# Fused attention and MLP on one Trainium2 core: turning the row sums with one or two DMAs, zeros through TensorE at the start, and a re-searched instruction order

## The chip, the core and the metric

The kernel runs on one core of a Trainium2 chip. The core has a matrix engine (TensorE, PE in the profile), a vector engine (VectorE, DVE), a scalar engine (ScalarE, ACT), GpSimd (POOL) and SyncE (SP). SyncE computes nothing here: it issues nearly all DMAs, one after the other, and SPq in the profile is its queue of issues. The metric is device time in microseconds (us) of one execution; lower is better.

## The reference, cut to what matters

Attention over 4 batches of 8 heads, 768 positions, 64 numbers per head, and then an MLP on its output. Three heads ("retrieval") see all earlier positions, the five others ("streaming") see a window of 64 and the first 4 positions ("sinks").

```python
scores = scale * np.matmul(q, k.transpose(0, 1, 3, 2))        # (4, 8, 768, 768)
mask = np.where(retrieval_head, causal, causal & (is_sink | in_window))
a = np.exp(np.where(mask, scores, -1e9) - max)
a = a / (np.sum(a, axis=-1, keepdims=True) + 1e-09)           # the row sums
x = np.matmul(a, v)  ->  (3072, 512)
h = x @ w_in                                                  # (3072, 2048)
g = h * (1.0 / (1.0 + np.exp(-beta * h)))
out = g @ w_out                                               # (3072, 512)
```

## The kernel before

**Units.** The work is cut into 8 units of 384 query rows: unit n is half u = n % 2 of batch b = n // 2. For each unit:

- q and k are loaded, cast to bf16 and turned so that the head's 64 numbers lie along the partitions. Units 0 to 2 turn them on TensorE (`transposes`); units 3 to 7 load whole blocks of 128 rows (`load_block`, tile `wf`), cast them on GpSimd (`cast_block`, tile `c`) and turn them by DMA (`turn_block`, the rows `DMA_TRANSPOSE QK<-c`, three per unit).
- `scores`: TensorE multiplies K by Q into PSUM (`sp`), `exps` (ScalarE) writes the exponentials `es`, `masks` (VectorE) zeroes what is masked.
- The row sums: matmuls of `es` with a 0/1 matrix that puts the sum of head h into one row of a PSUM bank. The bank has four groups of 32 rows (`QUARTERS` says which heads go into which group).
- From unit 2 on the sums take this way: `sums_d` (TensorE), `sums_copy` (PSUM to `sc`, mostly ScalarE), `sums_turn` (SyncE, DMAs `rec<-sc` that turn one row of 384 sums into 12 partitions of 32), `recips_d` (VectorE, RECIPROCAL `rec<-rec` of 96x32), `spread_w` (DMA `rd<-rec` to DRAM), `spread_r` (DMAs `R<-rd`, which spread each head's row over 64 partitions).
- `pv`: TensorE multiplies the exponentials by V; `norm` (VectorE) multiplies by `R` and writes `xT`.
- The MLP: `mm1` is 16 steps of 4 matmuls (`b<-xT,w_in`) for the first product, each followed by `swish_a` (ScalarE, tanh, tile `t`) and `swish_b` (VectorE, tile `gT`); `mm2` is 48 matmuls (`b<-w_out,gT`), in pieces of mostly 3, for the second. `out_copy` and `out_store` bring the result out (`osb`).

PSUM has a ring of four banks (`b`) and a ring of two double banks (`sp`). A bank of `mm1` is free again when its `swish_b` is done.

**Order.** No engine reorders anything: every engine runs its instructions in the order in which the program lists them. That order comes from a planner inside the kernel (`_Plan`), which is run once while the program is built. Each piece of work has an engine (or a choice of two), a cost in us, what it needs and gives, the buffers it takes and drops, and a number that ranks it (table `KEYS` per unit, `WEIGHTS` for constants and weights). The planner keeps a clock for each engine and one for the DMA bus, and lets the piece go next that can start first, the rank deciding between equals. For a DMA it says when the data has landed:

```python
            if dma:
                bus = max(bus, t + 0.5) + dma
                end = bus + 1.9
```

`GATES` holds back the loads of units 4 to 7 until a step of `mm1` of an earlier unit. `fill` puts matmuls that nothing reads into the gaps that the planner foresees on TensorE in unit 0; before, they multiply `ident`, which GpSimd and VectorE make first.

`sums_turn` finds runs of neighbouring rows within each group of 32 and issues one DMA for each run: 4 DMAs for an even unit, 6 for an odd one. The planner counts the two cases as 1.2 and 2.1 us of SyncE, and the landing does not hang on that cost.

All instructions are issued through one wrapper, so that the profile gives line 97 for nearly all of them; the tiles tell them apart.

Of the kernel before, what the change touches and what calls it, by code (L numbers as in the profile page):

```python
# [20 lines left out]
NQ = 384  # L21
# [4 lines left out]
RD = 2  # L26

QUARTERS = [[[1, 0], [2, 3], [4, 5], [6, 7]], [[0], [2], [6], [1, 3, 4, 5, 7]]]
# [3 lines left out]
    0: dict(lq=[-165.82, -155.72, -191.56, -178.1], lv=-145.25, C=[-65.39, -131.87, -41.89, -86.23],  # L32
            T=[-109.96, -88.07, -75.65, -67.05], Q=[-124.12, -146.02, -158.63, -111.34],
            cv=[-109.51, -97.53, -83.51], vs=-53.78, vk=-41.5,
            B=[-171.91, -59.89, -207.95, -67.25, -159.55, -110.28],
            E=[-142.81, -104.85, -52.78, -71.02, -207.86, -95.09],
            M=[-53.11, -45.88, -146.62, -152.03, -119.89, -106.16], S=-59.43, PV=[-123, -87.28], X=-92.41,
            F=[-125.92, -113.74, -33.78, -38.27], G=[11.96, 26.88, -25.34, -2.08], H=-153.06, sb=-40.97,
            K=[-58.1, -167.89, -89.9]),
    1: dict(lq=[-152.51, -123.51, -105.94, -134.66], lv=-99.01, C=[-154.83, -128.04, -9.58, -43.56],  # L40
            T=[-55.41, -182.82, -90.82, -169.77], Q=[-57.13, -132.73, -146.37, -81.96],
            cv=[-116.44, -38.55, -150.04], vs=-86.92, vk=-176.99,
            B=[-111, -108.66, -43.08, -108.9, -127.65, -131.33, -50.32, -14.84, -72.5, -21.72, -31.87],
            E=[-129.13, -134.44, -75.3, -47.48, -146.38, -120.46, -64.22, -105.37, -86.8, -132.54, -52.04],
            M=[-145.43, -115.22, -24.07, -114.07, -90.59, -74.79, -21.74, -185.38, -44.07, -45.06, -103.18],
            S=-126.37, PV=[-94.57, -58.91], X=-46.47, F=[-65.81, 2.22, 13.77, -8.12], G=[22.7, 27.98, 33.64, 49.4],
            H=-97.43, sb=-115.4),
    2: dict(lq=[-32.34, 36.54, -11.23, -37.8], lv=21.15, C=[21.76, 11.26, -63.87, 8.43],
            T=[-8.17, -63.33, -9.18, -36.89], Q=[-77.34, -70.04, -74.1, -11.35], cv=[-3.16, 145.7, 184.27], vs=-0.61,
            vk=19.6, B=[-74.54, -33.32, 1.69], E=[-49.81, -78.93, -15.93], M=[-72.26, 2.59, 8.17], S=-31.69,  # L50
            PV=[-16.56, -12.55], X=-38.15, F=[35.42, 13.85, -71.4, 21.4], G=[29.86, 37.66, 64.38, 29.32], R=-84.72,
            K=[-23.72, -47.63, 38.74]),
    3: dict(lq=[23.68], lv=34.32, C=[77.98, -33.67, 15.45], T=[-84.21, -89.69, 27.29], Q=[-43.91, -30.77, 1.18],
            cv=[104.3, 50.32, 139.71], vs=42.23, vk=26.7, B=[-53.03, 29.98, -28.16, -37.77, 10.22, 4.83],
            E=[-14.1, -109.92, 21.88, -3.59, -53.97, -8.41], M=[20.61, 15.21, -101.39, -28.76, 42.21, -8.5],
            S=-25.99, PV=[-52.29, 15.39], X=1.64, F=[-11.21, -21.04, 59.39, 24.49], G=[50.31, 79.24, 78.85, 95.19],
            R=-55.88),
    4: dict(lq=[0.64], lv=72.19, C=[-185.84, 18.49, -88.24], T=[51.44, -0.36, -78.85], Q=[30.04, -109.4, 26.76],
            cv=[9.73, -29.73, 29.61], vs=-1.89, vk=-78.57, B=[3.16, -9.02, -8.62], E=[-83.78, 54.42, 25.91],
            M=[37.95, 3.78, 19.61], S=47.2, PV=[68.33, 74.41], X=95.05, F=[79.33, 77.62, 52.17, 81.21],  # L60
            G=[100.92, 90.46, 90.81, 122.12], R=59.63, K=[-79.06, 20.85, -57.69]),
    5: dict(lq=[-54.23], lv=41.02, C=[-30.79, -100.17, 18.04], T=[-83.52, -0.48, -92.08], Q=[-76.69, -62.07, 36.64],
            cv=[-4.25, 32.39, 34.09], vs=72.24, vk=22.86, B=[27.07, 60.21, 46.43, -4.09, 55.17, -17],
            E=[50.88, -80.34, -97.23, -10.62, -15.3, 15.32], M=[83.6, -25.66, 72.38, 57.39, 68.27, -18.07], S=-7.32,
            PV=[88.41, 70.24], X=25.45, F=[93.13, -7.52, 67.58, 105.49], G=[112.06, 162.66, 102.69, 165.88],
            R=-23.19),
    6: dict(lq=[71.77], lv=-38.06, C=[-52.91, -57.88, 33.52], T=[56.65, -66.66, 25.11], Q=[-0.48, 30.2, -72.44],
            cv=[114.59, 24.4, 118.72], vs=61.5, vk=-61.89, B=[30.8, 69.89, 63.92], E=[45, -9.65, 73.65],
            M=[25.73, 56.3, 69.63], S=22.31, PV=[51.83, 110.46], X=52.04, F=[89.21, 129.45, 134.18, 72.91],
            G=[221.97, 189.97, 171.77, 186.22], R=134.28, K=[-4.2, 53.02, 30.27]),  # L70
    7: dict(lq=[77.55], lv=33.7, C=[-63.72, 57.49, 135.17], T=[-74.45, -13.02, -50.08], Q=[-15.93, -1.82, 53.36],
            cv=[38.13, 102.79, -30.27], vs=170.92, vk=47.74, B=[64.28, -10.97, 44.28, -0.69, 65.07, 43.28],
            E=[-97.6, 7.48, -19.53, 39.61, -51.31, -12.41], M=[161.75, 134.38, -44.81, 3.6, 63.97, 41.6], S=86.05,
            PV=[123.5, 45.3], X=51.72, F=[115.9, 95.83, 106.35, 147.7], G=[152.64, 132.66, 103.11, 188.88], R=-29.36),
}
WEIGHTS = dict(li=[-109.35, -92.93, -97.63, -84.5], lo=[-60.41, -56.12, -88.76, -77.95],
               ci=[-66.33, -100.62, -61.95, -70.77], co=[-53.12, -5.13, -24.02, -40.24], mask=[-76.97, -136.12],
               esel=-109.74, sel=-114.05, sink=-109.74, table=-90.21, masks=-135.98, beta=-73.84)
GATES = [32, 46, 56, 66]
# [23 lines left out]
class _Plan:  # L103
# [16 lines left out]
    def run(self):  # L120
# [11 lines left out]
        while any(left.values()):  # L132
# [62 lines left out]
def kernel(  # L195
# [69 lines left out]
    low = consts.tile([128, 1], F32, name="low")  # L265
    warm = consts.tile([128, 1], F32, name="warm")
# [24 lines left out]
    def const_masks():  # L291
        pool.memset(mask_c, 1.0)
        aff(mask_c, -1, 1, 0, 128)
        pool.memset(odd, 1.0)
        aff(odd, -1, 1, W, W)
        aff(odd, 1, -1, -1, W)
        pool.memset(even, 1.0)
        aff(even[0:W], -1, 1, 0, W)
        aff(even[W:2 * W], 1, -1, -1, W)

# [155 lines left out]
    def load_beta():  # L456
        held["beta"] = rp.tile([FO, 128], F32, name="beta", bufs=1)
        act.dma_start(out=held["beta"], in_=moe_beta.rearrange("(fo fi) -> fo fi", fi=128))
# [149 lines left out]
    BURST_COST = [[0.33, 0.36, 0.75], [0.33, 0.33, 0.4, 0.5, 0.65, 0.18]]  # L608
# [39 lines left out]
    def sums_d(x):  # L648
# [4 lines left out]
        for heads in QUARTERS[x.u]:  # L653
            ops = []
            for h in heads:
                e8 = esel[:, XH.index(h), :, :].rearrange("p a b -> p (a b)")
                if RETR[h]:
                    ops += [(e8, q0, n, e) for (kb, q0, n, e) in x.work[h]]
                else:
                    ops.append((e8, 0, NQ, x.work[h]))  # L660
            if not all(RETR[h] for h in heads):
                ops.append((esel_k.rearrange("p a b -> p (a b)"), q1, NQ - q1, x.esk[0:96, q1:NQ]))
            assert ops[0][1:3] == (0, NQ)
            todo.append(ops)
# [35 lines left out]
    def spread_r(x):  # L700
        x.R = rp.tile([128, NP, NQ], F32, name="R", bufs=RINGS["R"])
        src = x.rd[:]
        for i in range(2):
            sp.dma_start(
                out=x.R[i * D:(i + 1) * D],
                in_=bass.AP(src.tensor, src.offset + i * NQ, [[0, D], [2 * NQ, NP], [1, NQ]]))
# [114 lines left out]
    def attention(n, key, early):  # L821
# [15 lines left out]
        if n >= TD:  # L837
            for i in range(2):
                add(key["lq"][0] + 0.1 * i, "sp", 3.0, lambda i=i: load_block(x, i), dma=3.9, needs=gate,
# [5 lines left out]
            for j in range(TU):  # L845
                add(key["T"][j], "sp", 1.25, lambda j=j: turn_block(x, j), dma=0.7,
# [4 lines left out]
        for j in range(TU):  # L851
# [3 lines left out]
            elif j == 0:  # L855
                add(key["lv"], "sp", 3.0, lambda: [load_v(x, j, sp) for j in range(TU)], dma=3.9, needs=gate,
# [199 lines left out]
```

## Time and profile before

| what | us |
|---|---|
| runs: median of 3 (lowest, highest) | 256.96 (255.67, 258.22) |
| the profiled execution | 256.75 |
| its span, first to last instruction | 255.0 |
| TensorE busy | 230.1 (90%) |
| ScalarE busy | 143.9 (56%) |
| VectorE busy | 139.3 (55%) |
| GpSimd busy | 74.8 (29%) |
| packets of SyncE's hardware queue, share of 16 engines' span | 72.3% |

The span leaves 1.7 us of the execution's time outside. In the rows of a timeline stand the start, the length of the stretch that was merged into the row, the engine, the tiles (out<-in) with their shape, the count, and in brackets how long the engine stood idle before it and who released it. In a table of windows each engine has its busy time and its count of instructions, and PEclk is the share of full clock that TensorE was granted.

### The profile page before, as it was taken

Reading aid. Unit: us, or ns where it says so; the run is one execution under the profiler, and the core shown is the slowest. Engines: PE = TensorE matmul, PEld = TensorE weight load, DVE = VectorE, ACT = ScalarE, POOL = GpSimd, SP = SyncE. Lnnn points to the kernel's source line nnn. Section 1 sums busy time; section 2 is a strip of 40 time slices with the busy share of each in tenths; the row PEclk is TensorE's granted clock in tenths of the full one; section 3 lists DMA queues with packets and bytes.
Section 4 is the critical chain, followed back from the end, with each engine's and each line's share of the span. In section 5 each row is a group of like instructions: output and inputs, shape, how many; then the busy total and the mean of one; then the engine's idle time right before and its main releaser. Section 6 shows DMA issues by size and latency. Waiting matters only on the chain.

```text
span 255.0 us, 5440 instructions
## 1 busy us (share of the span) xinstructions
PE 230.1 (90%) x2103; PEld 125.5 (49%) x2103; DVE 139.3 (55%) x308; ACT 143.9 (56%) x239; POOL 74.8 (29%) x166
## 2 busy tenths in 40 slices
PE   3887999899989999699779959999999899999994
PEld 3645575555435454355334535555544446555441
DVE  4799798787005648236455726637753356566000
ACT  2698957794046974436467326518895254666110
POOL 6245857795800351124124300256000000000000
PEclk9999999999999999999999997999999999999999
DMA  7999999999776985999989929997216033101122
GB/s 204 265 319 316 205 337 332 362 216 195 134 171 197 229 167 121 193 181 238 183 172 211 197 40 155 220 223 194 47 17 154 31 99 85 41 0 43 41 82 82
DMA packets 91119, 42.72 MB, mean 167 GB/s; under 512 B 74693, under 2 KB 83925, under 8 KB 91093
## 3 DMA queue, kind: packets, MB, share of 16 engines
q1 hardware_dynamic: 89973, 41.58, 72.3%
q10 hardware_dynamic: 1120, 0.79, 1.0%
q8 instruction: 16, 0.26, 0.4%
q14 instruction: 10, 0.08, 0.1%
HBM read 31.99 MB, written 6.37 MB: 150 GB/s over the span
## 4 chain that ended last, share of the span: by engine, by line
PE 50%; DMA 21%; SPq 14%; POOL 6%; DVE 4%; issue 2%; ACT 2%; DVEq 0%; POOLq 0%; ACTq 0%
PE b L97 44%; SPq L97 14%; PE sp L97 6%; DMA wf<-in_moe_w_in_dram 6%; DMA wf<-in_v_dram 4%; DMA q2f<-in_q_dram 4%; DMA rec<-sc 3%; DMA wf<-in_moe_w_out_dram 3%; POOL w_out L97 2%; POOL vb L97 1%; DMA QK<-c 1%; DVE gT L97 1%; POOL w_in L97 1%; POOL vs L97 1%; ACT t L97 1%
## 5 line engine op out<-in xcount | busy, mean ns | idle before, releaser
L97 PE MATMUL b<-xT,w_in 128*128 128x384 bf16 x512 | 92.3, 330 | 5.0 <-DVE gT L97 4.4
L97 ACT ACTIVATE t<-b,beta_h 128x384 f32<-128x384 f32 x128 | 73.3, 582 | 37.1 <-PE b L97 23.6
L97 PE MATMUL b<-w_out,gT 128*128 128x512 bf16 x384 | 91.5, 380 | 1.6 <-DVE gT L97 1.6
L97 DVE SCALAR_TENSOR_TENSOR gT<-t,b 128x384 bf16<-128x384 f32 x128 | 69.0, 550 | 27.7 <-ACT t L97 22.2
L97 PEld LDWEIGHTS <-w_in 128*128 128x128 bf16 x512 | 49.3, 99 | 43.1 <-issue 10.0
L97 ACT ACTIVATE es<-sp 128x768 bf16<-128x768 f32 (+1 forms) x68 | 50.6, 793 | 18.1 <-PE sp L97 17.8
L97 PEld LDWEIGHTS <-gT 128*128 128x128 bf16 x384 | 35.7, 98 | 42.7 <-issue 2.5
L97 POOL CAST c<-wf 128x256 bf16<-128x256 f32 x60 | 23.0, 426 | 48.2 <-DMA wf<-in_q_dram 31.4
L97 ACT ACTIVATE osb<-b 128x512 f32<-128x512 f32 x18 | 10.6, 596 | 37.2 <-PE b L97 35.6
L97 PE MATMUL sp<-QK 64*64 64x128 bf16 (+6 forms) x420 | 19.8, 245 | 8.3 <-DMA QK<-c 5.5
L97 PEld LDWEIGHTS <-QK 64*64 64x64 bf16 (+1 forms) x420 | 10.6, 104 | 20.4 <-issue 14.4
L97 DVE TENSOR_TENSOR es<-es,mask_s 128x768 bf16<-128x768 bf16 (+1 forms) x24 | 13.3, 566 | 12.8 <-ACT es L97 12.4
L97 POOL CAST vb<-wf 128x512 bf16<-128x512 f32 x18 | 10.7, 616 | 27.1 <-DMA wf<-in_v_dram 27.1
L97 DVE TENSOR_TENSOR xT<-sp,R 128x768 bf16<-128x768 f32 x12 | 11.1, 954 | 12.5 <-PE sp L97 9.5
L97 PE MATMUL sp<-es,vb 128*64 128x64 bf16 (+3 forms) x228 | 15.6, 241 | 0.0
L97 DVE TENSOR_TENSOR es<-es,mask_c 128x256 bf16<-128x256 bf16 (+2 forms) x32 | 11.9, 389 | 5.7 <-ACT es L97 5.2
L97 DVE RECIPROCAL rec<-rec 96x32 f32<-96x32 f32 x6 | 2.1, 349 | 20.3 <-DMA rec<-sc 20.3
L97 POOL CAST w_in<-wf 128x512 bf16<-128x512 f32 x16 | 10.0, 666 | 8.6 <-DMA wf<-in_moe_w_in_dram 8.6
L97 PEld LDWEIGHTS <-vb 128*64 128x64 bf16 x228 | 11.8, 111 | 1.2
L97 PE MATMUL sp<-es,vs 128*64 128x64 bf16 x120 | 11.0, 196 | 0.0
L97 POOL CAST w_out<-wf 128x512 bf16<-128x512 f32 x16 | 10.0, 676 | 2.7 <-DMA wf<-in_moe_w_out_dram 2.6
L97 PEld LDWEIGHTS <-vs 128*64 128x64 bf16 x120 | 9.2, 111 | 1.6 <-issue 1.4
(74 smaller groups left out, 136.1 us busy)
## 6 DMA issues: line engine op xcount, KB each, us to landing
out_dram<-osb SPq DMA_DIRECT2D x24, 256.0 KB
wf<-in_v_dram SPq DMA_DIRECT2D x18, 256.0 KB
R<-rd SPq DMA_DIRECT2D x12, 384.0 KB
wf<-in_moe_w_out_dram SPq DMA_DIRECT2D x4, 1024.0 KB
wf<-in_q_dram SPq DMA_DIRECT2D x15, 256.0 KB
wf<-in_k_dram SPq DMA_DIRECT2D x15, 256.0 KB
wf<-in_moe_w_in_dram SPq DMA_DIRECT2D x4, 768.0 KB
q2f<-in_q_dram SPq DMA_DIRECT2D x12, 192.0 KB
```

The costliest lines, as they stand in the source:

```text
L97: ins = f(*a, **k)
```

## The change

**The sums' rows at constant steps.** `QUARTERS` and the new `ROWS` place head i of a group at row 16*i (even units) or row i (odd units) of its group of 32; the sums of an even unit then lie at rows 0, 16, 32, ... 112, one constant step, and those of an odd unit at 0, 32, 64 and 96 to 100. One DMA turns the first, two the second. The heads' order in `rec` and `rd` becomes `ORDER`; for odd units `spread_r` then needs three DMAs where two did. In the 0/1 matrix `one` (a window of which puts a sum into any row) and `own_k` (the sinks' part) take the place of `esel` and `esel_k` from unit 2 on; the first two units keep the old ones, and `own_k` is made on VectorE by three memsets and ten small casts.

```diff
-QUARTERS = [[[1, 0], [2, 3], [4, 5], [6, 7]], [[0], [2], [6], [1, 3, 4, 5, 7]]]
+QUARTERS = [[[1, 0], [2, 3], [4, 5], [6, 7]], [[2], [6], [0], [3, 5, 7, 1, 4]]]
+ROWS = [16, 1]
+ORDER = [[1, 0, 2, 3, 4, 5, 6, 7], [2, 6, 0, 3, 5, 7, 1, 4]]
...
         x.rec = rp.tile([8 * CR, 32], F32, name="rec")
-        for g, heads in enumerate(QUARTERS[x.u]):
-            at = sorted(XH.index(h) for h in heads)
-            while at:
-                n = 1
-                while n < len(at) and at[n] == at[0] + n:
-                    n += 1
-                sp.dma_start(out=x.rec[at[0] * CR:(at[0] + n) * CR, :],
-                             in_=x.sc[32 * g + at[0]:32 * g + at[0] + n, :].rearrange("p (c n) -> p c n", n=32))
-                at = at[n:]
+        for p, step, c, n in ([(0, 16, 0, 8)], [(96, 1, 3, 5), (0, 32, 0, 3)])[x.u]:
+            sp.dma_start(out=x.rec[c * CR:(c + n) * CR, :],
+                         in_=x.sc[p:p + (n - 1) * step + 1:step, :].rearrange("p (c n) -> p c n", n=32))
```

**Zeros from the first us.** A tile `blank` (a corner of an `xT` buffer) is zeroed by VectorE; TensorE begins with 25 matmuls of it (`fill_first`), and `fill` multiplies `blank` instead of `ident` where it uses the matmul form. `const_ident` moves ahead of the masks.

```diff
+    def const_blank():
+        dve.memset(blank, 0.0)
...
-        for _ in range(int(held["gap"] / 0.13)):
+        for _ in range(int(held["gap"] / 0.14)):
             if dst.dtype == BF16:
                 pe.transpose(dst, ident, ident)
             else:
-                pe.matmul(dst, ident, ident, start=True, stop=True)
+                pe.matmul(dst, blank, blank, start=True, stop=True)
+
+    def fill_first():
+        held["gap"] = 3.6
+        fill(bank("fill")[:, 0:128])
...
-    add(-110, "pool", 1.0, const_ident, gives=[("const", "ident")])
+    add(-310, "pool", 1.0, const_ident, gives=[("const", "ident")])
```

**The planner.** It now holds SyncE back when its queue is full (the last line of the piece below), lets a landing hang on the cost of the issue, and has new costs: the turned sums 0.75 and 1.5 us, the blocks of q, k and v 2.1 us of SyncE and 3.6 us of bus (3.0 and 3.9 before), the DMA transposes 1.28 and 1.3 (1.25 and 0.7), `spread_r` 1.33 and 2.0 (0.9).

```diff
             if dma:
-                bus = max(bus, t + 0.5) + dma
+                bus = max(bus, t + (0.5 if dma > 0.2 else cost)) + dma
                 end = bus + 1.9
+                now[e] = max(now[e], bus - 2.8)
...
-            add(key["R"] + 0.1, "sp", [1.2, 2.1][u], lambda: sums_turn(x), needs=[("sum_s", n)], gives=[("sum_t", n)], dma=0.1,
+            add(key["R"] + 0.1, "sp", [0.75, 1.5][u], lambda: sums_turn(x), needs=[("sum_s", n)], gives=[("sum_t", n)], dma=0.2,
```

**New ranks.** All of `KEYS`, `WEIGHTS` and `GATES` (`[32, 46, 56, 66]` becomes `[32, 46, 59, 72]`). A line of 80 or so:

```diff
-            S=-126.37, PV=[-94.57, -58.91], X=-46.47, F=[-65.81, 2.22, 13.77, -8.12], G=[22.7, 27.98, 33.64, 49.4],
+            S=-128.61, PV=[-143.2, -36.76], X=-22.83, F=[-4.3, -12.64, -36.76, 14.76],
```

The counts on TensorE stay: 2103 matmuls, 58 of them fills, in both programs. The order moves nearly everywhere; three places follow.

SyncE's queue in the second half of batch 1 (unit 3), from the loads of unit 4 to the transposes of unit 4 and the turned sums' way back, before:

```order
L97 DMA wf<-in_v_dram 128x8x64 x3
L97 DMA rec<-sc 12x1x32 x4
L97 DMA rec<-sc 36x1x32
L97 DMA rec<-sc 12x1x32
L97 DMA out_dram<-osb 128x512
L97 DMA_TRANSPOSE QK_106<-c 128x8x128 x3
L97 DMA rd<-rec 96x32
```

and now:

```order
L101 DMA wf<-in_v_dram 128x8x64 x3
L101 DMA out_dram<-osb 128x512
L101 DMA rec<-sc 60x1x32
L101 DMA rec<-sc 36x1x32
L101 DMA_TRANSPOSE QK_109<-c 128x8x128 x3
L101 DMA rd<-rec 96x32
L101 DMA wf<-in_q_dram 128x8x64 x3
L101 DMA R<-rd 64x2x384 x2
L101 DMA R<-rd 64x1536
```

Six issues ahead of the transposes became two, the store of one output tile went ahead of them, and the spreading behind has three DMAs. Unit 5 has the same pattern.

VectorE around the reciprocal of unit 5's sums, with `xT` of unit 4 before it and the `gT` of unit 4's first product behind it, before:

```order
L97 TENSOR_TENSOR xT<-sp_2406,R 128x768
L97 COPY vs<-vb 64x1536
L97 COPY vs<-vb 64x1024
L97 COPY vs<-vb 64x512
L97 TENSOR_TENSOR xT<-sp_2429,R 128x768
L97 RECIPROCAL rec<-rec 96x32
L97 SCALAR_TENSOR_TENSOR gT<-t,b_2509 128x384
L97 SCALAR_TENSOR_TENSOR gT<-t,b_2516 128x384
```

and now:

```order
L101 TENSOR_TENSOR xT<-sp_2431,R 128x768
L101 TENSOR_TENSOR xT<-sp_2405,R 128x768
L101 SCALAR_TENSOR_TENSOR gT<-t,b_2509 128x384
L101 SCALAR_TENSOR_TENSOR gT<-t,b_2516 128x384
L101 RECIPROCAL rec<-rec 96x32
L101 SCALAR_TENSOR_TENSOR gT<-t,b_2526 128x384
```

The reciprocal, which waits for SyncE's DMAs, stood ahead of all `gT` of unit 4 and now stands behind the first two of them; the copies of V left this place.

At the same place in the program, the scores of unit 6 now begin after 11 of the 16 steps of unit 4's first product, and no longer after all 16 and the `pv` of unit 5. On TensorE there stood between the sums of unit 5 and the first scores of unit 6 12 matmuls of unit 3's second product, 64 of unit 4's first, 27 of unit 4's second and the `pv` of unit 5; now there stand 12, 44, 6 and no `pv`. Between the same sums and the first scores of unit 7 there are now 28 steps of first product, 42 matmuls of second product, the `pv` of unit 5 and unit 6's scores and sums.

GpSimd's first instructions, before:

```order
L97 MEMSET mask_c 128x128
L97 ISA
L97 AFFINE_SELECT mask_c<-mask_c 128x128
L97 MEMSET odd 128x64
L97 AFFINE_SELECT odd<-odd 128x64 x2
L97 MEMSET even 128x64
L97 AFFINE_SELECT even<-even 64x64 x2
L97 MEMSET warm 128x1
L97 MEMSET identf 128x128
L97 AFFINE_SELECT identf<-identf 128x128 x2
```

and now:

```order
L101 MEMSET warm 128x1
L101 MEMSET identf 128x128
L101 ISA
L101 AFFINE_SELECT identf<-identf 128x128 x2
L101 MEMSET mask_c 128x128
L101 AFFINE_SELECT mask_c<-mask_c 128x128
```

The identity comes first and the masks after it. On VectorE the cast of the identity is the first instruction and the memset of `blank` the second, so the zeros begin one memset after the identity is there; then TensorE has 25 fills with `blank`, 14 with `ident`, and the first transposes of unit 0, where it had 40 fills with `ident` before them.

More of the change, by code (lines that the diff above doesn't have):

```diff
@@ L265 @@
     low = consts.tile([128, 1], F32, name="low")
+    blank = xp.tile([128, NP, NQ], BF16, name="xT")[:, 0, 0:128]
+    one = consts.tile([128, 63], BF16, name="one")
+    own_k = consts.tile([96, 5, 32], BF16, name="own_k")
     warm = consts.tile([128, 1], F32, name="warm")
@@ L299, in const_masks, with const_own @@
         aff(even[W:2 * W], 1, -1, -1, W)
+    def const_blank():
+        dve.memset(blank, 0.0)
+    def const_own():
+        dve.memset(one, 0.0)
+        dve.memset(one[:, 31:32], 1.0)
+        dve.memset(own_k, 0.0)
+        for u in range(2):
+            for g, heads in enumerate(QUARTERS[u]):
+                for i, h in enumerate(heads):
+                    if not RETR[h]:
+                        pi = [h in p for p in PAIRS].index(True)
+                        dve.tensor_copy(out=own_k[:, 4 if u else g, ROWS[u] * i:ROWS[u] * i + 1],
+                                        in_=sel_k[0:96, pi - 1, PAIRS[pi].index(h):PAIRS[pi].index(h) + 1])
     def const_zero():
@@ L855, in attention @@
             elif j == 0:
-                add(key["lv"], "sp", 3.0, lambda: [load_v(x, j, sp) for j in range(TU)], dma=3.9, needs=gate,
+                add(key["lv"], "sp", 2.1, lambda: [load_v(x, j, sp) for j in range(TU)], dma=3.6, needs=gate,
                     gives=[("vf", n, j) for j in range(TU)], take=[("wf", (n, 0), TU)])
@@ L943, in attention @@
             add(key["R"] + 0.3, "sp", 0.4, lambda: spread_w(x), needs=[("rec", n)], gives=[("rd", n)], dma=0.1, drop=[("rec", n)])
[L944 removed]
+            add(key["R"] + 0.4, "sp", [1.33, 2.0][u], lambda: spread_r(x), needs=[("rd", n)], gives=[("R", n, t) for t in range(NP)], dma=4.0,
                 take=[("R", n, 2)])
@@ L1003 @@
         add(WEIGHTS["mask"][u], "dve", 0.9, lambda u=u: const_mask_s(u), needs=[("const", "m")], gives=[("const", "mask", u)])
+    add(-300, "dve", 0.15, const_blank, gives=[("const", "blank")])
+    add(-300, "pe", 2.8, fill_first, needs=[("const", "blank")], gives=[("const", "fill")], take=[("b", "fill", 1)], drop=[("b", "fill")])
+    add(WEIGHTS["own"], "dve", 1.5, const_own, needs=[("const", "sink")], gives=[("const", "own")])
     add(-109, "dve", 0.5, const_zero, gives=[("const", "zero")])
```

132 lines of the change are left out of this document (68 added, 64 removed).

## The prediction

> **What bounds the kernel now.** I read the page first: busy times, then the slices.
>
> ```profile
> span 255.0 us, 5440 instructions
> ...
> PE 230.1 (90%) x2103; PEld 125.5 (49%) x2103; DVE 139.3 (55%) x308; ACT 143.9 (56%) x239; POOL 74.8 (29%) x166
> ...
> PE   3887999899989999699779959999999899999994
> ...
> PEclk9999999999999999999999997999999999999999
> ```
>
> TensorE is busy for 230.1 of 255.0 us and every other engine for little over half. A change that takes no matmuls away can win only what TensorE stands idle or runs slowly: 24.9 us of idle, and the one slice (the 25th, at 153 to 159 us) in which its clock was low. So the next view is TensorE's own waits, by releaser.
>
> ```profile
> PE b L97 <- DVE gT L97: 6.0, 4, 2.7
> PE sp L97 <- DMA QK<-c: 5.5, 4, 2.4
> PE b L97 <- DVE ident L97: 4.2, 1, 4.2
> ```
>
> Columns: us in total, times, longest. These three are 15.7 of the 24.9 us; the rest are the tail behind the last matmul, which the change doesn't touch, and waits below a us. What stands behind the first line is seen in the timeline around the longest such wait.
>
> ```profile
> 145.09 2.12 PE L97 MATMUL b<-w_out,gT 128*128 128x512 bf16 x9
> 145.20 0.48 ACT L97 COPY sc<-b 128x384 f32<-128x384 f32 x1 [2.51 <-PE b L97]
> 145.70 4.79 SPq L97 DMA_DIRECT2D rec<-sc  x6
> 147.04 2.11 PE L97 MATMUL b<-xT,w_in 128*128 128x384 bf16 x12
> 148.99 0.81 PE L97 MATMUL b<-w_out,gT 128*128 128x512 bf16 x3
> 151.67 0.35 DVE L97 RECIPROCAL rec<-rec 96x32 f32<-96x32 f32 x1 [4.74 <-DMA rec<-sc]
> 152.48 5.74 PE L97 MATMUL b<-xT,w_in 128*128 128x384 bf16 x24 [2.68 <-DVE gT L97]
> ```
>
> The sums of unit 5 are copied at 145.20, six DMAs are issued until 150.49, the reciprocal runs 1.18 us later. VectorE waits 4.74 us at the reciprocal with every `gT` of unit 4 queued behind it, so no bank comes free and TensorE stops for 2.68 us. The starts also give the prices of PE work: 9 second-product matmuls in 1.95 us (0.217 each), 12 first-product ones in 1.95 us (0.65 a step of four).
>
> ```profile
> 150.00:160.00 10.00, 7.52 (x36) 4.06 (x36) 5.57 (x11) 5.46 (x10) 0.00 (x0) 0.83 0.97 137
> ```
>
> Column seven is the granted clock: 0.83 over 10 us, 1.7 us of full speed lost right behind that gap.
>
> **The change, part by part.**
>
> *Fewer DMAs for the sums.* From copy to end of reciprocal an odd unit takes 145.20 to 152.02, 6.8 us. At 4.79 / 6 = 0.80 us an issue, two take 1.60, and the chain is 0.50 + 1.60 + 1.18 + 0.35 = 3.6 us: 3.2 less. For an even unit:
>
> ```profile
> 125.00 2.87 SPq L97 DMA_DIRECT2D rec<-sc  x4
> 129.26 0.35 DVE L97 RECIPROCAL rec<-rec 96x32 f32<-96x32 f32 x1 [4.45 <-DMA rec<-sc]
> 130.08 0.39 PE L97 MATMUL b<-w_out,gT 128*128 128x512 bf16 x1 [1.56 <-DVE gT L97]
> ```
>
> Four issues at 0.72 become one: 2.15 less. Waits of 2.68 (odd) and 1.56 (even) are both shorter than what goes, and the other two are 6.0 - 2.68 - 1.56 = 1.76 together. **All 6.0 us go, and with the gap its 1.7 us of half clock.** What is late next at unit 5 is tanh: by the new order the reciprocal stands behind the second `gT`, and the third `gT` needs 12 second-product matmuls and three steps (2.6 + 1.95 us) and a tanh, which is later than the 3.6 us of the chain. Whether one DMA of 96 rows lands later than four of 24 no row shows; between 1.18 us (odd) and 1.39 (even: 127.87 to 129.26) for the landings there is little to add.
>
> *The same on SyncE.* 30 issues of `rec` become 9, and `R` has three more: 18 fewer. What was queued behind them gains:
>
> ```profile
> 63.17 3.36 SPq L97 DMA_DIRECT2D rec<-sc  x4
> 66.64 4.12 SPq L97 DMA_TRANSPOSE QK<-c  x3
> 72.63 0.50 PE L97 MATMUL sp<-QK 64*128 64x384 bf16 x4 [1.26 <-DMA QK<-c]
> 92.71 4.79 SPq L97 DMA_DIRECT2D rec<-sc  x6
> 98.17 4.10 SPq L97 DMA_TRANSPOSE QK<-c  x3
> 104.15 0.52 PE L97 MATMUL sp<-QK 64*64 64x192 bf16 x22 [2.35 <-DMA QK<-c]
> 126.11 0.31 PE L97 MATMUL sp<-QK 64*64 64x64 bf16 x8 [1.40 <-DMA QK<-c]
> ```
>
> At units 3 and 4 the transposes start as soon as the `rec` issues (and one store) are through, so the wait there is the queue's. Three of four issues at 0.84 (2.5 us) and 3.2 us exceed the waits of 1.26 and 2.35: **3.6 us go.** At unit 5 (1.40, and 0.5 left of the 5.5) no `rec` stands right ahead; the queue is 3.2 us ahead from unit 3's sums, if the blocked loads between let that through. Between 0 and 1.9 I take 0.7.
>
> *Start.*
>
> ```profile
> 3.81 0.30 DVE L97 CAST ident<-identf 128x128 bf16<-128x128 f32 x1 [2.53 <-POOL identf L97]
> 4.17 3.68 PE L97 MATMUL b<-ident 128*128 128x128 bf16 x40 [4.17 <-DVE ident L97]
> 4.34 0.55 POOL L97 CAST c<-q2f 128x384 bf16<-128x384 f32 x1
> 7.68 0.33 PE L97 MATMUL b<-ident,c 128*128 128x128 bf16 x3
> 7.88 0.51 POOL L97 CAST c<-q2f 128x384 bf16<-128x384 f32 x1 [2.54 <-DMA q2f<-in_q_dram]
> 8.82 0.51 POOL L97 CAST c<-q2f 128x384 bf16<-128x384 f32 x1 [0.43 <-DMA q2f<-in_q_dram]
> ```
>
> Forty fills hold TensorE until 7.68, though the first data are cast at 4.89. With the masks (some 2 us) behind it the identity is there at about 2.1, the zeros begin near 2.3, and 39 fills at 3.5 / 40 = 0.09 us end near 5.9: 1.8 us earlier. But the third and fourth loads still land at 7.88 and 8.82, and work on them had been late by 1 us at most. Bounds 0 and 1.8; I take 1.0, nearer to what the loads allow.
>
> *Added.* `own_k`'s ten casts and three memsets on VectorE, in unit 0's first product. Nearest rows, ten such casts and copies in a row:
>
> ```profile
> 5.96 0.17 DVE L97 CAST esel_k<-sel_k 96x4 bf16<-96x4 f32 x1
> 6.56 0.14 DVE L97 COPY sink_own<-sel_k 96x1 f32<-96x1 f32 x1
> ```
>
> 0.74 us; with the memsets 0 (four banks hide it) to 1.2 us; I take 0.3. The third `R` DMA is an issue of under a us on a queue that gains 3.2 at the same place: nothing.
>
> *New ranks and gates.* Gaps that no row of before shows can open where things moved closer. Two places are tight by the order: units 6 and 7.
>
> ```profile
> 123.25 1.46 PE L97 MATMUL b<-xT,w_in 128*128 128x384 bf16 x8
> 127.92 2.03 SPq L97 DMA_DIRECT2D wf<-in_v_dram  x3
> 144.19 2.70 POOL L97 CAST c<-wf 128x256 bf16<-128x256 f32 x6 [5.77 <-DMA wf<-in_k_dram]
> 158.71 1.33 SPq L97 DMA_TRANSPOSE QK<-c  x1
> 160.10 5.12 SPq L97 DMA_DIRECT2D wf<-in_q_dram  x3
> 174.72 4.04 SPq L97 DMA_TRANSPOSE QK<-c  x3
> ```
>
> Unit 6: after unit 5's sums TensorE now has 18 second-product matmuls and 11 steps, 3.9 + 7.15 = 11.0 us, to its scores. SyncE meanwhile: copy 0.5, two `rec`, a store that waits for an output tile (until about 3.9), two transposes at 1.37, `rd`, the third: 8.4, and 1.88 to land (102.27 to 104.15): 10.3. Slack 0.7 us. Unit 7: its loads follow three `R` at about 10.4; from load to landed transposes before took 160.10 to 178.76 and 1.88, 20.5 us, so 30.9, and up to 2 more for the v load that now stands between. TensorE has 28 steps (18.2), 42 second-product matmuls (9.1), and about 4.7 by my estimate for attention: 32.0. So between 1.1 us spare and 0.9 late. Bounds for both and all smaller places 0 and 8.5 us (below); I take 1.0 and 1.5, since slack under a us is no slack in a queue whose rows vary by as much.
>
> **Sum.** 255.0 - 6.0 - 1.7 - 3.6 - 0.7 - 1.0 + 0.3 + 2.5 = 244.8 us of span; 1.7 us lie outside, so 246.5 against the profiled execution's 256.75, which is 0.2 below the median of the runs shown.
>
> **Rivals.**
>
> *New waits for old (B).*
>
> ```profile
> L97 DVE TENSOR_TENSOR xT<-sp,R 128x768 bf16<-128x768 f32 x12 | 11.1, 954 | 12.5 <-PE sp L97 9.5
> ```
>
> Units 6 and 7, and `xT` (a product of 0.95 us on VectorE, while behind unit 5's `pv` now stand only 6 second-product matmuls, 1.3 us, before the step that needs it), open gaps of 2 to 3 us, one of them with half clock behind it: 5 to 8.5 us in place of 2.5. Time 249 to 252.5. For it: the slacks just worked out. Against: before, unit 6's casts were done at 146.89, 1.7 us after the copy of unit 5's sums began, so at unit 6 no load is short, only the queue.
>
> [...]
>
> *Issue time goes with rows (C).* If a DMA of 96 rows takes as long to issue as four of 24, SyncE gains nothing and the change doesn't do what it says: only the start and chance remain, 254 to 257. Against: `rec` pieces of 12 to 36 rows take 0.80 on the mean, those of 24 0.72 to 0.84.
>
> *Slower (D): loads released later and wanted earlier.* Unit 6's loads wait for step 11 of unit 3's first product instead of step 8 (123.25), and from there to its scores TensorE has some 25 us of work by the same prices. Before, the last transpose landed at 161.9, 38.7 us after release. Unit 7: 33 us before, 23 now. If the chain takes as long again, TensorE waits 13 and 10 us: 269. It decides when the two late by more than 13 us together (above 259). Against: of the 38.7 us the transposes waited long after the casts were done (146.89); from the v load at 127.92 to there are 19.0 us, and 3.2 for a transpose and its landing give 22.2, below 25.
>
> **How the numbers follow.** Forecast 0.70; B 0.17; C 0.07; D 0.06. One per cent (254.4 and 259.5 against 256.96) is about what a measurement of this kernel can tell from no change. Faster: forecast, nearly all of B, 0.86; same: C and edges, 0.08; slower: D, 0.06. The lower end takes the good bounds, 1.9 instead of 0.7 at unit 5, 1.8 instead of 1.0 at the start, and 2.5 of tightness gone: 246.5 - 4.5 = 242. The upper end takes in most of B: 252.
>
> **What would show it.** TensorE's wait for `gT` falls from 6.0 to under 1, that for `QK` from 5.5 to under 3, of what is left most at units 6 and 7; VectorE's wait at the reciprocal (20.3 us before in all) falls to a few us; SyncE shows one or two `rec` issues in a row, 0.7 to 0.8 each; no slice at half clock; the first `b<-ident,c` at about 6 us. I am wrong if `rec` issues grow with their rows, if waits for `QK` at units 6 and 7 exceed 5 us, or if the first 50 us lose what the start wins.

## The result and the profile after

| | before | after |
|---|---|---|
| median of 4 runs each, us (lowest, highest) | 256.31 (255.41, 258.22) | 244.59 (243.35, 246.62) |
| the profiled execution, us | 256.75 | 243.35 |
| its span, us | 255.0 | 241.6 |

The ratio is 0.9541, with a 95% interval of 0.9448 to 0.9634. The page of the kernel after, the same lines as before:

```profile
span 241.6 us, 5401 instructions
...
PE 227.1 (94%) x2082; PEld 125.4 (52%) x2103; DVE 136.0 (56%) x311; ACT 144.4 (60%) x242; POOL 79.4 (33%) x174
...
PE   6779999799999999999999999999999999999993
...
PEclk9997999999999999999999999999999999999999
```

From the ninth slice (48 us) on TensorE is full to the tail. The low clock at 153 us is gone, and another stands in the fourth slice. TensorE's waits (us in total, times, longest), and VectorE's at the reciprocal:

```profile
PE b L101 <- DVE xT L101: 2.4, 2, 2.2
...
PE sp L101 <- DVE QK L101: 1.6, 3, 0.8
...
PE b L101 <- DVE gT L101: 0.3, 1, 0.3
```

```profile
DVE rec L101 <- DMA rec<-sc: 4.1, 2, 3.9
```

The wait for `gT` fell from 6.0 to 0.3. The wait for `QK<-c`, 5.5 before, is not in the list at all. VectorE's wait at the reciprocal fell from 20.3 (its row below) to 4.1. The 2.2 for `xT` is the very start: the zeros wait for their tile. What SyncE pays for the sums (ns, shortest/median/longest), after and then before:

```profile
L101 SPq DMA_DIRECT2D rec<-sc x9: 697/790/917, 62.7 to 190.6; - x9
```

```profile
L97 SPq DMA_DIRECT2D rec<-sc x30: 628/727/877, 63.2 to 201.7; - x30
...
  DVE rec L97: 20.3, 6
```

Thirty issues became nine, and one that turns 36 to 96 rows costs hardly more than one of 12 to 36. The timeline at unit 5, the place of the 2.68 us gap:

```profile
138.29 0.48 ACT L101 COPY sc<-b 128x384 f32<-128x384 f32 x1 [2.51 <-PE b L101]
139.26 1.71 SPq L101 DMA_DIRECT2D rec<-sc  x2
142.06 2.69 SPq L101 DMA_TRANSPOSE QK<-c  x2
142.25 1.20 DVE L101 SCALAR_TENSOR_TENSOR gT<-t,b 128x384 bf16<-128x384 f32 x2 [3.19 <-ACT t L101]
143.37 0.34 DVE L101 RECIPROCAL rec<-rec 96x32 f32<-96x32 f32 x1
143.63 2.42 DVE L101 SCALAR_TENSOR_TENSOR gT<-t,b 128x384 bf16<-128x384 f32 x4
```

The reciprocal has no bracket: its data were there when VectorE came to it, behind two `gT`.

**Where the time came from.** The first step of the first product starts here:

```profile
25.66 2.60 PE L97 MATMUL b<-xT,w_in 128*128 128x384 bf16 x15
```

```profile
5.76 0.33 PE L101 MATMUL b<-ident,c 128*128 128x128 bf16 x3
...
25.96 2.29 PE L101 MATMUL b<-xT,w_in 128*128 128x384 bf16 x13
```

So up to there the kernel after is 0.3 us later, though its first transposes come 1.9 us earlier (5.76 against 7.68); the stretch of low clock in the fourth slice lies between (see "The clock near 20 us"). From there to the end it takes 241.6 - 25.96 = 215.6 us against 229.3: 13.7 less. Of these, 5.7 are the wait for `gT`, 5.5 that for `QK` and 1.7 the half clock; 0.8 is left, for smaller waits that were not followed up.

### The profile page after: what moved, and what is told of

It reads as the page before. It is cut to its first block, busy times and chain, and to the rows that moved or that the text cites. A ratio compares the mean times of both kernels' runs of the same rounds, so it can differ in the third digit from the quotient of the medians.

```text
span 241.6 us, 5401 instructions
## 1 busy us (share of the span) xinstructions
PE 227.1 (94%) x2082; PEld 125.4 (52%) x2103; DVE 136.0 (56%) x311; ACT 144.4 (60%) x242; POOL 79.4 (33%) x174
## 4 chain that ended last, share of the span: by engine, by line
PE 73%; DMA 11%; SPq 3%; POOL 3%; DVE 3%; issue 2%; ACT 1%; another core or an unknown queue 1%; ACTq 1%; POOLq 0%
PE b L101 63%; PE sp L101 10%; DMA wf<-in_moe_w_out_dram 5%; DMA wf<-in_moe_w_in_dram 4%; SPq L101 3%; DMA k2f<-in_k_dram 2%; POOL c L101 1%; POOL w_in L101 1%; DVE es L101 1%; DVE gT L101 1%; POOL w_out L101 1%; ACTq L101 1%; ACT es L101 1%; ACT osb L101 0%
## 5 line engine op out<-in xcount | busy, mean ns | idle before, releaser
L101 PE MATMUL b<-xT,w_in 128*128 128x384 bf16 x512 | 90.4, 326 | 0.4
L101 PE MATMUL b<-w_out,gT 128*128 128x512 bf16 x363 | 86.6, 379 | 2.1 <-issue 1.6
L101 PEld LDWEIGHTS <-w_in 128*128 128x128 bf16 x512 | 48.8, 98 | 37.0 <-issue 2.3
L101 ACT ACTIVATE es<-sp 128x768 bf16<-128x768 f32 (+1 forms) x68 | 50.7, 797 | 10.5 <-PE sp L101 10.3
L101 POOL CAST c<-wf 128x256 bf16<-128x256 f32 x60 | 21.5, 407 | 44.3 <-DMA wf<-in_q_dram 23.2
L101 PEld LDWEIGHTS <-QK 64*64 64x64 bf16 (+1 forms) x420 | 10.3, 104 | 14.9 <-issue 10.8
L101 PE MATMUL sp<-es,vb 128*64 128x64 bf16 (+3 forms) x228 | 16.3, 248 | 0.0
L101 DVE TENSOR_TENSOR es<-es,mask_c 128x256 bf16<-128x256 bf16 (+2 forms) x32 | 10.8, 349 | 9.0 <-ACT es L101 8.4
L101 DVE TENSOR_TENSOR es<-es,mask_s 128x768 bf16<-128x768 bf16 (+1 forms) x24 | 11.8, 497 | 6.2 <-ACT es L101 5.6
L101 POOL CAST vb<-wf 128x512 bf16<-128x512 f32 x18 | 10.9, 628 | 13.2 <-DMA wf<-in_v_dram 9.5
L101 POOL CAST w_in<-wf 128x512 bf16<-128x512 f32 x16 | 9.3, 614 | 12.2 <-DMA wf<-in_moe_w_in_dram 12.2
L101 DVE TENSOR_SCALAR osb<-b 128x512 f32<-128x512 f32 x6 | 4.1, 680 | 16.1 <-DMA out_dram<-osb 12.4
L101 POOL COPY vs<-vb 64x1536 bf16<-64x1536 bf16 (+2 forms) x10 | 12.0, 1208 | 0.3
```

Source lines behind the costliest of these rows:

```text
L101: ins = f(*a, **k)
```

## The experiments

The theory: the time came from the shorter chain on SyncE. The rivals: the new order and ranks did it; the start did it. Ratios are to the kernel before, run on the same chip within the same group of runs.

### The rows alone

The kernel before with one part of the change. Instructions and their order stay on every engine but for the sums' DMAs, the third `R` DMA of odd units, the 0/1 matrices that the sums are multiplied with, and `own_k`, which VectorE makes behind unit 1's reciprocal.

```diff
+ROWS = [16, 1]
+ORDER = [[1, 0, 2, 3, 4, 5, 6, 7], [2, 6, 0, 3, 5, 7, 1, 4]]
...
+        for p, step, c, n in ([(0, 16, 0, 8)], [(96, 1, 3, 5), (0, 32, 0, 3)])[x.u]:
+            sp.dma_start(out=x.rec[c * CR:(c + n) * CR, :],
+                         in_=x.sc[p:p + (n - 1) * step + 1:step, :].rearrange("p (c n) -> p c n", n=32))
```

> The kernel before with the sums' rows of the change alone: the same instructions in the same order on every engine, but one or two DMAs where four or six turn the sums, three where two spread the rows of an odd unit, and own_k made on VectorE behind unit 1's reciprocal. Theory (the chain from sums to reciprocal was too long by the issues on SyncE, and that held VectorE and the transposes up): TensorE's waits for gT (6.0 us) and for QK at units 3 and 4 (3.6 us) go, with the 1.7 us of half clock behind the longest, and 0 to 1.9 us at unit 5; 243.5 to 245.5 us, near the whole of the change's 11.7 us. Rival (the new order and ranks brought the time, the DMAs only fitted in): the old order keeps most of its waits, 252 to 256 us, and the wait for gT stays above 3 us.

Measured: 245.41 us against 258.03, ratio 0.9499 (0.9454 to 0.9543). This is all of the change's gain. TensorE's waits:

```profile
PE b L99 <- DVE ident L99: 4.2, 1, 4.2
...
PE sp L99 <- DMA QK<-c: 1.5, 2, 1.1
...
PE b L99 <- DVE gT L99: 0.8, 1, 0.8
```

The waits for `gT` and those for `QK` at units 3 and 4 are gone in the order of before, and the PEclk line is 9 in all 40 slices. The 0.8 for `gT` is a new wait at 40 us, right behind the 13 small instructions that make `own_k`. What is left for `QK` stands at unit 5, where it was 1.40 and 0.47 before:

```profile
123.46 0.31 PE L99 MATMUL sp<-QK 64*64 64x64 bf16 x8 [1.12 <-DMA QK<-c]
124.16 0.45 PE L99 MATMUL sp<-QK 64*64 64x128 bf16 x15 [0.39 <-DMA QK<-c]
```

So the new order is not needed for the gain.

### The pieces back, and half of them

The kernel after in its own order, with four or six DMAs again, and with two or four.

```diff
-        for p, step, c, n in ([(0, 16, 0, 8)], [(96, 1, 3, 5), (0, 32, 0, 3)])[x.u]:
+        for p, step, c, n in ([(32 * g, 16, 2 * g, 2) for g in range(4)],
+                              [(96, 1, 3, 1), (97, 1, 4, 3), (100, 1, 7, 1)] + [(32 * g, 32, g, 1) for g in range(3)])[x.u]:
```

> The kernel after, its order unchanged, with the sums turned by four DMAs (even units) or six (odd units) again. Theory (chain length): each chain is 2.2 us (even) or 3.0 us (odd) longer on SyncE and the transposes start that much later; VectorE's wait at the reciprocal grows from 4.1 to over 12 us, and the waits for QK and gT come back, 5 to 12 us in all: 249 to 256 us. Rival (order alone): the new order puts the reciprocal behind two gT and hides the longer chain; 244 to 246 us.

> The kernel after, its order unchanged, with two DMAs for an even unit's sums and four for an odd unit's. Theory (chain length, with the slack that the order leaves): each chain is 0.7 us (even) or 1.5 us (odd) longer; the time lies between the kernel after and the one with four and six, and if the order has about 1.5 us of slack at these places it is within 2 us of the kernel after: 244.5 to 247 us. If the cost went with each issue on SyncE alone, without slack, it would be half of what four and six cost.

Measured: 254.39 us, ratio 0.9845 (0.9792 to 0.9898), with the pieces back; 247.84 us, 0.9623 (0.9556 to 0.9691), with half of them. Waits with the pieces back:

```profile
PE b L101 <- DVE gT L101: 4.9, 5, 2.5
```

```profile
DVE rec L101 <- DMA rec<-sc: 15.8, 6, 4.6
```

Waits for `gT` are back, and VectorE waits 15.8 us at the reciprocal where it waited 4.1. So the new order without the new rows keeps about a third of the gain (1.55% of 4.6%, with an interval from 1.0 to 2.1%), and the chain's length decides in it too. Half of the pieces cost 0.8 to 1.1% over the kernel after (0.951 to 0.954), all of them 3.0 to 3.3%: a quarter to a third, with intervals that also allow the half.

These times hold a beginning that scatters. Up to the sums of unit 2, the first that SyncE turns, the three kernels are the same program, and yet these sums begin at different times in the kernel after, with half of the pieces and with all of them:

```profile
57.88 0.67 PE L101 MATMUL b<-es,one 128*32 128x384 bf16 x12 [0.33 <-DVE gT L101]
61.51 0.67 PE L101 MATMUL b<-es,one 128*32 128x384 bf16 x12 [0.82 <-DVE gT L101]
59.36 0.67 PE L101 MATMUL b<-es,one 128*32 128x384 bf16 x12 [0.30 <-DVE gT L101]
```

From there to the end the profiled executions take 183.7, 187.6 and 193.2 us: 3.9 more for 9 more issues, and 9.5 more for 21 (1.7 of it half clock behind the longest wait). Read so, the price goes roughly with the number of issues, and slack of 1.5 us in the order is not seen.

### The issues, behind

In the old order with the new rows, SyncE issues three or four small DMAs more behind those of the sums. The reciprocal is early (VectorE waits 6.3 us there in all, 5.5 with the rows alone, 20.3 before), the queue as full as before.

```diff
+        for j in range([3, 4][x.u]):
+            sp.dma_start(out=idle[24 * j:24 * j + 12, :], in_=x.sc[32 * j:32 * j + 1, :].rearrange("p (c n) -> p c n", n=32))
```

> The old order with the sums' rows, and behind the one or two DMAs that turn the sums three (even units) or four (odd units) more on SyncE that turn one row each into a tile that nothing reads. So the reciprocal comes as early as with the rows alone, while SyncE's queue is as full as in the kernel before. Theory (two paths: 6.0 + 1.7 us through VectorE's wait at the reciprocal, 3.6 to 5.5 us through the transposes behind the issues): the wait for gT stays under 1.5 us, the wait for QK comes back to 4 to 6 us; 3 to 5.5 us more than the rows alone, 0.962 to 0.972 of the kernel before. Rival 1 (only the reciprocal counted): within 1 us of the rows alone, 0.947 to 0.954. Rival 2 (SyncE's queue is all of it): 0.99 to 1.0.

Measured: 254.23 us, ratio 0.9881 (0.9824 to 0.9938). The price of a full queue alone is 8.0 us of span over the rows alone (252.1 against 244.1), and 3.8% by the ratios, not 3 to 5.5 us. Waits, clock and the new place:

```profile
PE sp L99 <- DMA QK<-c: 4.1, 4, 1.9
PE sp L99 <- DVE xT L99: 2.8, 2, 2.3
```

```profile
100.00:110.00 10.00, 7.93 (x53) 3.52 (x53) 5.25 (x15) 3.25 (x5) 0.45 (x2) 0.86 1.01 195
110.00:120.00 10.00, 9.70 (x116) 5.11 (x116) 4.33 (x8) 3.48 (x5) 3.11 (x9) 0.97 1.05 198
```

```profile
166.16 2.36 DVE L99 COPY KS<-QK 64x4 bf16<-64x4 bf16 x5 [6.06 <-DMA QK<-c]
168.55 1.82 DVE L99 TENSOR_TENSOR xT<-sp,R 128x768 bf16<-128x768 f32 x2
169.56 0.34 PE L99 MATMUL sp<-QK 64*128 64x384 bf16 x2 [2.28 <-DVE xT L99]
```

Waits for `QK` are 2.6 us more than with the rows alone, for `xT` 2.8; the granted clock costs 1.4 + 0.3 = 1.7: together 7.1. A wait of 0.9 for `w_in` at 31 us is no price of the issues, since the first of them goes out at 66.9 us. From the sums of unit 2 on (61.87 here, 61.33 with the rows alone) the two take 190.2 and 182.8 us, so the price behind that point is 7.4.

The wait for `xT` is the late transposes again, by another way. VectorE stands 6.06 us at a copy that reads them, and `xT`, whose end frees TensorE's bank, is queued behind it.

Neither my theory's sum nor rival 1 holds; rival 2 lies nearest. So the split that I read from the waits (7.7 us through the reciprocal, 4.3 through the queue) is wrong. With the reciprocal's path alone freed 1.2% is won (0.6 to 1.8%), some 3 us; from the sums of unit 2 on, where the kernel before takes 195.8 us, it is 5.6 of the 13.0 us that the rows win. The queue holds the rest. The other way round, a late reciprocal with an empty queue, was not run, so what the reciprocal's path would cost alone is not shown. The change shortens both with one edit.

### The start

First with the planner told of it, as the change does, on the kernel before:

```diff
+    add(-300, "dve", 0.15, const_blank, gives=[("const", "blank")])
+    add(-300, "pe", 2.8, fill_first, needs=[("const", "blank")], gives=[("const", "fill")], take=[("b", "fill", 1)], drop=[("b", "fill")])
```

> The kernel before with the start of the change alone: the tile of zeros, 25 matmuls of it first, and the identity ahead of the masks. Theory (VectorE and ScalarE bound the first 25 us, and the third and fourth loads land when they did): the first transposes come 1.5 to 2 us earlier, the first step of the first product no more than 0.5 us earlier; 255.5 to 257.5 us, no change that can be measured. Rival (the start goes through): all of the 1.8 us, 254 to 255 us.

Measured: 264.36 us, ratio 1.0234 (1.0176 to 1.0292), a miss for both. The planner's clocks shifted and it listed much of the program in another order by the old ranks. Two new waits show it:

```profile
116.73 4.22 PE L97 MATMUL b<-xT,w_in 128*128 128x384 bf16 x12 [5.79 <-DVE xT L97]
155.94 0.50 PE L97 MATMUL sp<-QK 64*128 64x384 bf16 x2 [6.40 <-DVE xT L97]
```

So the order was kept by hand: the identity, the tile of zeros and the 25 matmuls are issued before the planned program, and 26 fills are left out of it. This goes on the kernel before, and on the rows alone.

```diff
+    const_ident()
+    blank = xp.tile([128, NP, NQ], BF16, name="xT")[:, 0, 0:128]
+    dve.memset(blank, 0.0)
...
+    for _ in range(25):
+        pe.matmul(zeros[:, 0:128], blank, blank, start=True, stop=True)
```

> The kernel before in its own order, with the start of the change alone: the identity first on GpSimd and VectorE, 25 matmuls of zeros first on TensorE, 26 of the 40 fills behind them left out. Theory (VectorE and ScalarE bound the first 25 us): the first transposes 1.5 to 1.9 us earlier, the first step of the first product at most 0.5 us earlier; the time as before, or 1 to 1.7 us more where the idle time that TensorE gains lets its clock fall. Rival (the start goes through): 1.8 us less, and then the 6.3 us that the start cost with the planner told of it came from the order alone.

> The old order with the sums' rows and the new start, so all of the change but the planner's costs and the ranks. Theory (rows bring all, start nothing): as with the rows alone, 0.947 to 0.955 of the kernel before, within 0.7 us of the kernel after in either direction. Rival (the start goes through): 1.8 us below the rows alone, 0.943, faster than both kernels.

Measured: 257.96 us, ratio 1.0008 (0.9964 to 1.0052), and 246.8 us, 0.9572 (0.9504 to 0.9639). The start wins nothing that can be measured. It does get through 20 us, contrary to my reason: on the kernel before the first product begins at 24.53, not 25.66, and with the rows at 24.05, where the rows alone have 26.43 (0.7 of this difference is only that the 40 fills ended later in that execution). Then comes a new wait, here with the rows:

```profile
24.05 2.76 PE L99 MATMUL b<-xT,w_in 128*128 128x384 bf16 x16
...
30.21 3.56 PE L99 MATMUL b<-xT,w_in 128*128 128x384 bf16 x12 [1.99 <-POOL w_in L99]
```

```profile
29.31 1.96 POOL L99 CAST w_in<-wf 128x512 bf16<-128x512 f32 x3 [1.33 <-DMA wf<-in_moe_w_in_dram]
```

```profile
30.00:35.00 5.00, 4.79 (x74) 2.89 (x75) 1.66 (x3) 1.75 (x3) 3.51 (x7) 0.68 0.97 278
```

The second block of `w_in` has not landed, and 1.6 us of half clock stand behind the wait; without the rows the wait is 2.1 us. Is it the load that gives the start back? Two kernels with a quarter of `w_in`'s bytes tell, one without and one with the new start:

```diff
-                           [[d_ff, n], [128 * d_ff, tiles], [1, 2 * FS]])
+                           [[d_ff, n], [128 * d_ff, tiles], [1, 128]])
```

> The rows alone, but of each block of w_in only the first quarter of its columns is loaded and cast four times (the first product is computed with repeated columns). It is the comparison for the next kernel. Theory (the loads of w_in limit only a faster start): within 1 us of the rows alone, 0.946 to 0.954 of the kernel before. Rival (DMA traffic holds up the whole beginning): 1 to 4 us less.

> The rows and the new start in the old order, with w_in loaded and cast as in the kernel before this one (the first product is computed with repeated columns). Theory (a start that is 1.1 to 2.4 us earlier runs into casts of w_in that wait for loads on full DMA engines): TensorE's wait of 2.0 us for w_in goes, the second step group follows the first, and the time is 1.5 to 2.4 us below the one with light loads alone. Rival (the start is used up by VectorE and ScalarE or by later waits): within 0.7 us of it.

Measured: 245.57 us (0.9547, 0.9503 to 0.959), just above the theory's range, and 243.37 us (0.9464, 0.9423 to 0.9506). With light loads the start is worth 2.2 us. Its second group of steps, and that of the kernel without the new start:

```profile
28.62 2.12 PE L99 MATMUL b<-xT,w_in 128*128 128x384 bf16 x12
```

```profile
30.89 2.12 PE L99 MATMUL b<-xT,w_in 128*128 128x384 bf16 x12
```

In the old order the third block is loaded ahead of the second. A last kernel, with full loads, exchanges the two:

```diff
-lambda s=s, ld=ld: ld(s)
+lambda s=s, ld=ld, w=w: ld([0, 2, 1, 3][s] if w == "i" else s)
```

> The rows and the new start in the old order, with one exchange: in the old order the third block of w_in is loaded and cast ahead of the second, though the first product needs the second block first (its casts are those at 29.3 us, for which TensorE waits 2.0 us); here the two blocks change places on SyncE and GpSimd, and nothing else does. Theory (the start was won and given back at that block): the wait for w_in goes and with it the half clock behind it; 243 to 245 us on a chip with 257.5 before, 0.943 to 0.951, as with the light loads and as fast as or faster than the kernel after. Rival (the DMA engines bound the beginning, whatever block comes first; a wait for the third block comes in its place): 0.953 to 0.961, as with the rows and the start.

Measured: 245.03 us, ratio 0.9499 (0.9469 to 0.953). Its profiled execution took 247.5 us, with half clock from 18.8 and from 124.6 us, and is read for one thing only: the second group waits no longer.

```profile
29.62 2.12 PE L99 MATMUL b<-xT,w_in 128*128 128x384 bf16 x12
```

The time is within the theory's range, below the rival's and equal to the rows alone, but the intervals with and without the exchange overlap. So the exchange takes the wait away, yet the start still shows no gain over the rows alone (0.9499 for both): that this block is all that gives the start back is not shown with full loads. No kernel with the whole computation beats the change measurably.

### The clock near 20 us

In the kernel after the clock is halved from 18.9 to 22.3 us. Rows of its windows (second number: TensorE's busy time; 0.99 and 0.51: the clock), and of the longest wait in the first:

```profile
15.50:18.90 3.40, 1.86 (x40) 1.19 (x41) 3.39 (x11) 3.40 (x6) 1.65 (x2) 0.99 0.93 276
18.90:22.30 3.40, 3.40 (x53) 2.67 (x49) 2.79 (x7) 1.62 (x4) 0.00 (x0) 0.51 0.95 286
```

```profile
16.22 0.34 PE L101 MATMUL sp<-QK 64*128 64x384 bf16 x2 [0.82 <-DVE QK L101]
```

So 25 matmuls of zeros were put where TensorE idles before it, and the kernel after was run beside it.

```diff
+        more(ps[:, 0, 0:128], {(0, 0, 1): 12, (1, 0, 0): 2, (1, 0, 1): 5}.get((x.n, pi, ri), 0))
...
+            more(sm[:, 0:128], 6)
```

> The kernel after once more, as the comparison for the others of this group: 0.95 to 0.96 of the kernel before, with a stretch of 3.4 us at half clock near 19 us (mean clock 0.986 to 0.991).

> The kernel after with 25 more matmuls of zeros where TensorE idles between 12 and 19 us (12 before the scores of unit 0's first pair in its last round, 7 in the second pair's, 6 ahead of unit 0's sums). Theory (the clock is halved when a stretch of about 3.4 us holds too little TensorE work, 1.86 us between 15.5 and 18.9 us in the kernel after): no half clock before 30 us, mean clock 0.997 or more, and 1.2 to 1.7 us less than the kernel after. Rival (the clock follows something else, or the first 25 us are bound by VectorE and ScalarE, so that a full clock there wins nothing): within 0.5 us of the kernel after; or the zeros stand in the way and cost up to 1 us.

Measured: the kernel after 244.42 us, ratio 0.9513 (0.9468 to 0.9558), with a mean clock of 0.986 to 1.000; with the zeros 245.63 us, 0.9564 (0.952 to 0.9609), with a clock of 0.998 or more in all six runs. The clock came as the theory forecast it, the time did not: no gain shows, and the intervals overlap.

The half clock is not free at its place, though. VectorE (3.39 of 3.40 us busy) and ScalarE (3.40) bound the stretch before it, but in the stretch itself TensorE is the full engine (3.40; ScalarE 1.62). The kernel after was profiled a second time, in an execution at full clock. There the first product begins at 24.80 and not at 25.96, and of these 1.2 us 0.5 are left at the third group of steps (34.85 in the first execution), behind a wait for `gT`:

```profile
24.80 2.77 PE L101 MATMUL b<-xT,w_in 128*128 128x384 bf16 x16
...
34.37 2.12 PE L101 MATMUL b<-xT,w_in 128*128 128x384 bf16 x12 [0.73 <-DVE gT L101]
```

With the zeros the first product begins at 25.02, but the same third group waits for `w_in`:

```profile
36.15 2.12 PE L101 MATMUL b<-xT,w_in 128*128 128x384 bf16 x12 [0.85 <-POOL w_in L101]
```

The spans of the two executions of the kernel after differ by the same 0.5 us (241.6 and 241.1). That is less than its runs scatter: the two runs at full clock took 242.82 and 245.49 us, and the one at 0.986 took 244.46.

## Why the prediction was right, point by point

The forecast was 246.5 us, and 244.59 was measured; against the profiled execution it was 246.5 to 243.35, or 244.8 to 241.6 in span.

- **Fewer DMAs, the wait for `gT` (-6.0, -1.7): right about the wait.** 0.3 is left, at another place (57.88), and the rows alone and the pieces back show it from both sides. As the price of that path 7.7 us is too much: with it alone freed some 3 us were won (1.2%), and the queue kept the rest (the issues behind).
- **Waits for `QK` at units 3 and 4 (-3.6): right; at unit 5 (-0.7): too small.** All 5.5 went. My reason, that the blocked loads stand between unit 3's sums and unit 5's transposes, was not wrong: with the rows alone 1.5 of the 1.9 stays there, and in the new order with the pieces back 0.5. So the new order frees most of this place, and no term of the sum had that.
- **The start (-1.0): 0.3 later in the profiled execution.** The step that failed is "no slice at half clock", on which the term silently rests: the half clock at 19 us lies ahead of the first product. In the execution at full clock it begins at 24.80, 0.9 earlier than before, close to the 1.0. Whether these 0.9 us last to the end no run isolates; in the old order the start's gain goes into the second block of `w_in`, a load that I had not looked at (my reason named the third and fourth loads of q).
- **`own_k` (+0.3): not seen** among TensorE's waits of the kernel after; with the rows alone 0.8 stands behind it.
- **Tight places at units 6 and 7 (+1.0, +1.5): wrong, nothing.** No wait for `QK` is left there, and the chains that I reckoned came out: 10.9 us at unit 6 (10.3 forecast) and 31.1 at unit 7 (30.9), if landing takes the 1.88 us of before. At unit 6 the scores began at 149.32 and the transposes had landed, by this estimate, at 149.17. So slack under a us did hold, but by 0.2 us only, and that is luck as much as order.
- **"No slice at half clock": wrong.** One came at 19 us; it costs 1.2 us up to the first product and 0.5 at the end, between two executions.
- **The rivals.** B (249 to 252.5) and D (269) did not come. C, that issue time goes with the rows, fell by the row of `rec`: 790 ns against 727.
- The wait of VectorE at the reciprocal (a few us), the `rec` issues (0.7 to 0.8; the longest 0.92) and the first transposes (about 6 us) came as said.

The sum missed by 3.2 us of span. Mis-sized were the tight places (2.5 that did not come), unit 5 (1.2 more) and the start (0.3 later, not 1.0 earlier: 1.3 the other way); the 0.8 that went besides stood in no term, and the 0.3 of `own_k` and the 0.3 left of `gT` cancel.

## What to carry to other kernels

Where one queue issues everything in order, count the issues: here one that turns up to 96 rows cost 0.79 us in the median where four of 24 rows cost 2.87, and everything behind them, on the queue and on the engine that waits for the data, moved up (VectorE waited 5.5 us at the reciprocal with the rows alone, 20.3 before). Give a wait that two paths feed its price only by an experiment that frees one path alone; read from the waits, my two paths were 7.7 and 4.3 us, and with the first freed 7.4 were still to be paid. Where kernels are the same program up to some point, compare them from that point on: here their beginnings alone differed by 3.6 us between executions. An earlier start can be lost at the next resource in line (here the second block of weights), and a planner that is told a new cost without new ranks can lose more than the cost is about.

## What the runs showed of the hardware

No one length of idle gap marks where the clock fell in these runs. Half clock (0.50 from 153.64 to 157.05 us) followed a wait of 2.68 us in the kernel before, but none followed one of 2.35 us there (1.00 from 102.44 to 109.26), while in the kernel with the issues behind half clock did follow 1.91 us at the same place (0.50 from 107.11 to 110.52), and in the kernel after it came with no wait over 0.82 us in the 3.4 us ahead of it (0.51 from 18.9 to 22.3).

The rows below are stretches of 3.41 us. In the kernel before they are the stretch with most of the 2.35 us wait, the one with most of the 2.68 us wait, and the one behind that; then, with the issues behind, the stretch with the 1.91 us wait and the one behind it. The second number is TensorE's busy time, the third from the right the clock:

```profile
102.44:105.85 3.41, 1.70 (x28) 0.99 (x28) 0.46 (x1) 1.30 (x2) 0.00 (x0) 1.00 0.86 180
150.22:153.63 3.41, 1.15 (x8) 0.69 (x8) 1.71 (x4) 1.11 (x3) 0.00 (x0) 1.00 0.46 82
153.64:157.05 3.41, 3.41 (x12) 1.60 (x11) 1.71 (x4) 1.93 (x4) 0.00 (x0) 0.50 1.21 128
```

```profile
103.69:107.10 3.41, 1.34 (x28) 0.76 (x28) 0.78 (x6) 0.96 (x2) 0.00 (x0) 1.00 0.86 179
107.11:110.52 3.41, 3.41 (x9) 1.23 (x9) 1.12 (x2) 1.14 (x2) 0.97 (x3) 0.50 1.27 239
```

TensorE worked 1.15 and 1.34 us in the two stretches with half clock behind them, and 1.70 us in the one without. Its busy time does not tell the cases apart everywhere: from 15.5 to 18.9 us it was 1.86 us in the kernel after, with a clock of 0.51 in the 3.4 us behind, and 1.81 us in the second execution of the same kernel, with 1.00 behind. Of the six runs that the second execution belongs to, two had a mean clock of 1.000 and four one of 0.986 to 0.993. What decides between them is not shown.
